# Reordering loads, transposes and casts in three blocks of a chunked-attention + squared-ReLU FFN kernel

## The chip, the cores and the metric

The kernel runs on one core of one Trainium2 chip. The metric is the device time of one execution in microseconds (us); lower is better. PE is the matmul engine (TensorE), DVE is VectorE, ACT is ScalarE, POOL is GpSimd, and SP is the engine whose queue issues nearly all DMAs here.

## The reference

The inputs are `q`, `k`, `v` of shape (8, 8, 576, 64) = (batch B, heads H, tokens S, head size D) and two weights, all float32. Attention is cut into chunks of 64 tokens that do not see each other; the result, 4608 tokens of 512 values, goes through a feed-forward layer with a squared ReLU.

```python
scores = scale * np.matmul(q_c, k_c.transpose(0, 1, 2, 4, 3))      # q_c, k_c, v_c: (B, H, 9, 64, D)
scores = scores - np.max(scores, axis=-1, keepdims=True)
attn = np.exp(scores)
attn = attn / (np.sum(attn, axis=-1, keepdims=True) + 1e-09)
out = np.matmul(attn, v_c)
x = out.transpose(0, 2, 1, 3).reshape(B * S, H * D)                # 4608 x 512
h = np.maximum(x @ w_in, 0.0)                                      # w_in 512 x 2048
return (h * h @ w_out)                                             # w_out 2048 x 512
```

## The kernel before

**Groups and blocks.** The 4608 tokens are cut into 18 groups of 256 tokens (four chunks), and the groups into 9 blocks of two: block j holds groups 2j and 2j+1. The FFN of block j is computed on PE while the attention of block j+1 (`nxt`) is fitted between its matmuls and the inputs of block j+2 (`far`) are loaded, cast and transposed. So block 3 holds groups 6 and 7, block 4 groups 8 and 9, block 5 groups 10 and 11.

**Steps of one group g.**
- Loads, all on SP's DMA queue: `qk_pieces` (L106, L120) gives one q load of 512 KB and two k loads of 256 KB (whole groups); `v_pieces` (L148, L152) gives two `ve_sb` loads of 128 KB (even heads) and two or three `vo_sb` loads of 64 or 128 KB (odd heads).
- `C` = `cast_q` (L334) and `cast_k` (L341): q and k to bf16, on POOL for g < 8, on ACT from there. `CQ` and `CK` are the two apart.
- `TD` = `transpose_qk_dma` (L352): one DMA transpose, also on SP's queue, gives `qkT`.
- `SC` = `scores` (L375 matmuls on PE, one exp on ACT, L386).
- `AV` = `values` (L403 matmuls on PE; reciprocal L410 and product L411 on DVE give `x`).
- `XT` = `transpose_x` gives `xT`, which the FFN reads: for g < 6 eight transposes on PE (L430) and one copy (L435); from g = 6 a DMA transpose on SP's queue (L424).

**The FFN of a block.** First comes x @ w_in (`ffn_in` or `ffn_in_unit`: matmuls L607 and, in blocks 2 to 8, the products of `unit`, L494), with the ReLU on ACT (L571, L598) and squares on DVE, POOL or ACT. Then `ffn_out` (L664): seven products into two PSUM banks, `n` and `m`, with copies of a bank to SBUF between them: n1 (L728), n2 (L737), and the output part (L771), all on ACT. The second product into `n` must wait until n1 is copied, the third until n2 is copied.

**The order** is written out by hand (`tc.manual_schedule()`): each engine and the queue run their instructions in the order in which the Python code emits them. A block is a list of *slots*; a slot is one `yield` of the FFN generators (four matmuls of 512 columns, or eight of 256). `plan` says which attention step is emitted after which slot; in each slot of `go_slots` one more load of the list `loads` is emitted, ahead of that slot's steps; loads that are left go out after the block's last slot. Block 1 has 46 slots (32 of `ffn_in`, 14 of `ffn_out`), blocks 2 to 8 have 33 (19 and 14). `late_by` is 3 in the blocks 2 to 8. In block j = 3 the casts of group 11 thus stand at the slots 21 and 22, and the steps SC of the next block's groups at slot 8; the SC of groups 10 and 11 stand at slot 4 of block 4. The stores of outputs of blocks 1 and later are put back (`late`) and issued on SP's queue (L715).

**The queue.** Every DMA adds to one of eight semaphores in turn, and each waits for the landing of the DMA eight places ahead of it, so at most eight are in flight.

Of the kernel before, what the change touches and what calls it, by code (L numbers as in the profile page):

```python
# [17 lines left out]
def kernel(  # L18
# [31 lines left out]
    def is_whole(g):  # L50
        return chunks[g][0][0] == chunks[g][3][0]
# [38 lines left out]
    def runs(g):  # L90

        for t in range(2):
            (b, s), (b1, s1) = chunks[g][2 * t:2 * t + 2]
            if b == b1:
                yield t, 0, 2 * CH, b, s
            else:
                yield t, 0, CH, b, s
                yield t, CH, CH, b1, s1

    def qk_pieces(g):  # L100
        q_sb = in_pool.tile([128, 2, H, D], FP32, name="q_sb")
        k_sb = in_pool.tile([128, 2, H, D], FP32, name="k_sb")
        qk[g] = (q_sb, k_sb)

        def pairs(dst, src, p, m, b, s):
            return lambda: nc.sync.dma_start(  # L106
                out=dst.rearrange("p t h d -> p (t h d)")[p:p + m // 2, :].rearrange(
                    "p (h e) -> p h e", h=H),
                in_=src[b, :, s:s + m, :].rearrange("h (s i) d -> s h (i d)", i=2))

        if is_whole(g):
            yield pairs(q_sb, q, 0, GT, *chunks[g][0])
        else:
            for c in range(4):
                yield pairs(q_sb, q, c * CH // 2, CH, *chunks[g][c])
        if g < FIRST_DMA_T:
            yield pairs(k_sb, k, 0, GT, *chunks[g][0])
            return
        for t, p, m, b, s in runs(g):
            yield lambda t=t, p=p, m=m, b=b, s=s: nc.sync.dma_start(  # L120
                out=k_sb[p:p + m, t, :, :],
                in_=k[b, :, s:s + m, :].rearrange("h s d -> s h d"))
# [23 lines left out]
    def v_pieces(g):  # L146
        for t, p, m, b, s in runs(g):
            yield lambda t=t, p=p, m=m, b=b, s=s: nc.sync.dma_start(  # L148
                out=v_even[g % NV][p:p + m, t, :, 0:D],
                in_=v[b, 0::2, s:s + m, :].rearrange("h s d -> s h d"))  # L150
        for n, p, m, b, s in odd_loads[g]:
            yield lambda n=n, p=p, m=m, b=b, s=s: nc.sync.dma_start(  # L152
                out=v_odd[n % NO][p:p + m, :, 0:D],
                in_=v[b, 1::2, s:s + m, :].rearrange("h s d -> s h d"))

    def go(pieces):
        for f in pieces:
            f()
# [278 lines left out]
    C, CQ, CK, TD = cast_qk, cast_q, cast_k, transpose_qk_dma  # L437
    SC, AV, XT = scores, values, transpose_x
# [183 lines left out]
    def sum_quarters(out, in0, in1, op=ALU.add, half=slice(None)):  # L622
        return lambda _: add(nc.vector, out[:, half], in0[:, half], in1[:, half], op)
# [182 lines left out]
    def pieces(grps):  # L806
        for g in grps:
            yield from qk_pieces(g)
        for g in grps:
            yield from v_pieces(g)  # L810
# [62 lines left out]
    for j, grps in enumerate(blocks):  # L873
        nxt = blocks[j + 1] if j + 1 < len(blocks) else []
        far = blocks[j + 2] if j + 2 < len(blocks) else []
        plan = {}

        def at(slot, f, g):
            plan.setdefault(slot, []).append((f, g))

        if j == 0:
            loads, go_slots = pieces(far), range(17)
            at(28, sum_quarters(b11_p_b21, b11, b21), None)
            for slot, f in ((24, TA), (27, SC), (29, AV), (31, XT)):
                at(slot, f, nxt[0])
            at(31, TQ, nxt[1])
            at(31, TK, nxt[1])
            at(31, sum_quarters(b11_m_b22, b11, b22, ALU.subtract), None)
            phases = [first_ffn_in, ffn_out_by_ft(0)]
        elif j == 1:  # L890
            loads, go_slots = itertools.chain(*map(qk_pieces, far)), range(26, 48)
            for slot, f in ((4, SC), (8, AV), (12, XT)):
                at(slot, f, grps[1])
            for i, g in enumerate(nxt):
                for slot, f in ((16 + 4 * i, C), (21 + 4 * i, TD), (36 + i, SC), (38 + 2 * i, AV),
                                (41 + 2 * i, XT)):
                    at(slot, f, g)
            for i, g in enumerate(far):
                at(36 + 4 * i, C, g)
                at(42 + 3 * i, TD, g)  # L900
            at(2, sum_quarters(b11_p_b12, b11, b12), None)
            at(12, sum_quarters(b12_p_b22, b12, b22), None)
            at(20, sum_quarters(b21_p_b22, b21, b22), None)
            phases = [ffn_in(1, [(0, 256, FT_ORDER), (256, 256, FT_ORDER)]), ffn_out(1)]
        else:
            loads, go_slots = pieces(far), range(32)
            slots = {SC: (4, 4), AV: (7, 11), XT: (10, 14), C: (18, 22), TD: (20, 24)}
            if j == 3:
                slots.update({SC: (8, 8), AV: (10, 14), XT: (13, 17)})
                go_slots = [*range(6), *range(13, 17), *range(20, 32)]  # L910
            if not is_whole(nxt[0] if nxt else 0):
                slots.update({SC: (6, 8), AV: (10, 14), XT: (12, 16)})
            if j == 2:
                loads = itertools.chain(*map(v_pieces, nxt), loads)
                slots = {SC: (8, 10), AV: (12, 15), XT: (15, 18), C: (20, 23), TD: (22, 25)}
                go_slots = [*range(16), *range(25, 36)]
            late_by = 0
            if j in UNITS:
                late_by = 3
            if j == 2:  # L920
                slots.update({AV: (12, 16), XT: (15, 19)})
                go_slots = [*range(16), *range(28, 39)]
            elif j in UNITS:
                go_slots = range(35)
                if far and is_whole(far[0]):
                    go_slots = [*range(6), *range(13, 17), *range(23, 35)]
                slots.update({SC: (4, 4), AV: (8, 13), XT: (12, 17)})
                if j == 3 or not is_whole(nxt[0] if nxt else 0):
                    slots.update({SC: (8, 8), AV: (11, 16), XT: (14, 19)})
            for f in (SC, AV, XT):  # L930
                for i, g in enumerate(nxt):
                    at(slots[f][i], f, g)
            if j > 2 and far and is_whole(far[0]):
                for slot, f, i in ((16, CQ, 0), (18, CK, 0), (18, TD, 0), (18, CQ, 1),
                                   (19, CK, 1), (19, TD, 1)):
                    at(slot + late_by, f, far[i])
            else:
                for f in (C, TD):
                    for i, g in enumerate(far):
                        at(slots[f][i] + late_by, f, g)  # L940
            phases = [ffn_in_unit(j) if j in UNITS else ffn_in(j, [(0, BT, FT_ORDER)]),
                      ffn_out(j)]
        slot = 0
        for phase in phases:
            for _ in phase:
                if slot in go_slots:
                    for f in loads:
                        f()
                        break
                for f, g in plan.get(slot, []):  # L950
                    f(g)
                while late and (slot >= LATE_STORES.get(j, 99) or (j, slot) == (2, 9)):
                    late.pop(0)()
                slot += 1
        assert all(x < slot for x in plan), (j, slot, sorted(plan))
        go(loads)
        while late and j > 1:
            late.pop(0)()
# [30 lines left out]
```

## Time and profile before

| | |
|---|---|
| time, median of 3 runs | 280.36 us (279.69 to 280.68) |
| the profiled execution | 282.07 us, span of its instructions 280.3 us |
| PE busy | 269.5 us (96%), 3047 matmuls |
| DVE, ACT, POOL busy | 205.2, 155.7, 95.4 us |
| DMA | 57.11 MB; SP's queue fills 84.8% of 16 DMA engines' span |
| granted PE clock | 0.993 on the mean |

The views name a group of instructions by line, engine, operation and tiles (out<-in), and say after `<-` what ended the idle time before it. `SPq` rows are the issuing of a DMA by SP's queue: their duration is the time to issue, and the landing comes later. The busy digits are tenths of a slice of 7 us.

### The profile page before, as it was taken

Reading aid. Unit: us, or ns where it says so; the run is one execution under the profiler, and the core shown is the slowest. Engines: PE = TensorE matmul, PEld = TensorE weight load, DVE = VectorE, ACT = ScalarE, POOL = GpSimd, SP = SyncE. Lnnn points to the kernel's source line nnn. Section 1 sums busy time; section 2 is a strip of 40 time slices with the busy share of each in tenths; the row PEclk is TensorE's granted clock in tenths of the full one; section 3 lists DMA queues with packets and bytes.
Section 4 is the critical chain, followed back from the end, with each engine's and each line's share of the span. In section 5 each row is a group of like instructions: output and inputs, shape, how many; then the busy total and the mean of one; then the engine's idle time right before and its main releaser. Section 6 shows DMA issues by size and latency. Waiting matters only on the chain.

```text
span 280.3 us, 7376 instructions
## 1 busy us (share of the span) xinstructions
PE 269.5 (96%) x3047; PEld 186.2 (66%) x3047; DVE 205.2 (73%) x313; ACT 155.7 (56%) x262; POOL 95.4 (34%) x110
## 2 busy tenths in 40 slices
PE   6987999999999999899999999999999999999995
PEld 4642445788785678457855785578558855885684
DVE  0542704899888798689868795979589949786794
ACT  1544713787426765579265927583779185507710
POOL 2036868351043810172017301720190019003403
PEclk9997999999999999999999999999999999999999
DMA  6999999989999879999999999897699992204004
GB/s 230 234 337 336 303 347 243 310 223 214 181 223 170 208 234 205 246 272 235 204 212 267 219 186 294 190 153 165 152 295 224 180 274 39 40 22 130 0 0 152
DMA packets 141313, 57.11 MB, mean 204 GB/s; under 512 B 110368, under 2 KB 135200, under 8 KB 141280
## 3 DMA queue, kind: packets, MB, share of 16 engines
q1 hardware_dynamic: 140544, 54.67, 84.8%
q0 software_dynamic: 592, 1.84, 1.7%
q8 instruction: 24, 0.39, 0.6%
q10 hardware_dynamic: 144, 0.13, 0.1%
q14 instruction: 9, 0.07, 0.1%
HBM read 36.70 MB, written 9.44 MB: 165 GB/s over the span
## 4 chain that ended last, share of the span: by engine, by line
PE 50%; DVE 0%; issue 0%
PE ps_ffn L664 24%; PE ps_ffn L607 19%; PE ps_ffn L494 6%; PE ps_att L403 1%; PE ps_att L375 1%; DVE o_sb L769 0%
## 5 line engine op out<-in xcount | busy, mean ns | idle before, releaser
L607 PE MATMUL ps_ffn<-xT,w_in_bf 128*128 128x512 bf16 (+1 forms) x528 | 112.7, 357 | 2.9 <-POOL w_in_bf L166 2.0
L620 POOL TENSOR_TENSOR gT<-rl 128x512 bf16<-128x512 f32 x40 | 45.5, 1152 | 121.5 <-ACT rl L571 118.3
L607 PEld LDWEIGHTS <-w_in_bf 128*128 128x128 bf16 x528 | 50.9, 99 | 40.8 <-POOL w_in_bf L166 2.5
L664 PEld LDWEIGHTS <-w_st 128*128 128x128 bf16 x640 | 62.2, 98 | 7.7 <-issue 0.4
L571 ACT ACTIVATE rl<-ps_ffn 128x512 f32<-128x512 f32 x84 | 50.0, 596 | 30.4 <-PE ps_ffn L607 30.2
L620 DVE TENSOR_TENSOR w_st<-gT 128x2048 bf16<-128x2048 bf16 x40 | 47.4, 1219 | 6.0 <-ACT gT L574 5.9
L664 PE MATMUL ps_ffn<-w_out_bf,w_st 128*128 128x256 bf16 x384 | 45.1, 273 | 0.0
L620 DVE TENSOR_TENSOR gT<-rl 128x512 bf16<-128x512 f32 x30 | 20.7, 691 | 21.1 <-ACT rl L571 20.7
L664 PE MATMUL ps_ffn<-w_sum,w_st 128*128 128x256 bf16 x256 | 29.6, 273 | 0.2 <-ACT n L737 0.2
L664 PEld LDWEIGHTS <-gT 128*128 128x128 bf16 x256 | 24.7, 98 | 5.0 <-ACT gT L574 0.5
L602 DVE TENSOR_TENSOR gT<-rl 128x256 bf16<-128x256 bf16 (+1 forms) x41 | 18.5, 491 | 10.2 <-ACT rl L598 9.8
L598 ACT ACTIVATE rl<-ps_ffn 128x256 bf16<-128x256 f32 (+1 forms) x48 | 20.3, 455 | 9.6 <-PE ps_ffn L607 8.9
L511 DVE SCALAR_TENSOR_TENSOR gT<-rl 128x512 bf16<-128x512 f32 x21 | 23.2, 1103 | 0.4
L411 DVE TENSOR_TENSOR x<-ps_att,rec 128x512 bf16<-128x512 f32 x32 | 22.1, 691 | 1.1
L771 ACT COPY o_sb<-ps_ffn 128x512 f32<-128x512 f32 x7 | 4.1, 585 | 30.4 <-PE ps_ffn L664 30.4
L386 ACT ACTIVATE e<-ps_att 128x1024 bf16<-128x1024 f32 x16 | 15.8, 1023 | 5.4 <-PE ps_att L375 5.4
L494 PEld LDWEIGHTS <-w_dif 128*128 128x128 bf16 x140 | 13.1, 98 | 7.5
L664 PE MATMUL ps_ffn<-w_out_bf,gT 128*128 128x256 bf16 x128 | 15.6, 273 | 0.0
L664 PE MATMUL ps_ffn<-w_sum,gT 128*128 128x256 bf16 x128 | 15.3, 273 | 0.0
L166 POOL CAST w_in_bf<-w_st 128x1024 bf16<-128x1024 f32 (+1 forms) x9 | 8.7, 969 | 19.0 <-DMA w_st<-in_moe_w_in_dram 19.0
L620 DVE TENSOR_TENSOR w_st<-xT 128x1024 bf16<-128x1024 bf16 (+1 forms) x21 | 12.5, 652 | 2.8 <-DMA xT<-x 2.0
L781 PE MATMUL ps_ffn<-w_out_bf,gT 128*128 128x512 bf16 x64 | 14.5, 380 | 0.0
(82 smaller groups left out, 294.2 us busy)
## 6 DMA issues: line engine op xcount, KB each, us to landing
q_sb<-in_q_dram SPq DMA_DIRECT2D x16, 512.0 KB, 6.4
k_sb<-in_k_dram SPq DMA_DIRECT2D x24, 256.0 KB, 6.0
out_dram<-o_sb SPq DMA_DIRECT2D x12, 512.0 KB, 4.3
w_st<-in_moe_w_in_dram SPq DMA_DIRECT2D x8, 512.0 KB, 8.6
w_st<-in_moe_w_out_dram SPq DMA_DIRECT2D x8, 512.0 KB, 6.0
ve_sb<-in_v_dram SPq DMA_DIRECT2D x28, 128.0 KB, 3.2
vo_sb<-in_v_dram SPq DMA_DIRECT2D x21, 128.0 KB, 3.1
k_sb<-in_k_dram SPq DMA_DIRECT2D x4, 512.0 KB, 6.8
```

Of the source, the lines that this page charges most:

```text
L166: nc.gpsimd.tensor_copy(out=w_in_bf[:, :, i * 256 + c:i * 256 + c + n], in_=st[:, :, c:c + n])
L386: nc.scalar.activation(out=e_out, in_=s_in, func=AF.Exp, scale=scale)
L411: nc.vector.tensor_tensor(out=x[:, t].rearrange("p h a d -> p a h d"), in0=o[:, :, :, 0:D], in1=rec.to_broadcast([128, 2, n_hp, D]), op=AL ...
L494: nc.tensor.matmul(out=out[:, 256 * f:256 * f + 256], lhsT=a[:, d, 128 * f:128 * f + 128], rhs=b[:, :, d, :], start=(first and f == 0 and ...
L511: later.append(lambda: nc.vector.scalar_tensor_tensor(out=place_of(i, jj), in0=both(x), scalar=0.0, in1=both(x), op0=ALU.max, op1=ALU.mult))
L571: nc.scalar.activation(out=rl, in_=h, func=AF.Relu)
L598: nc.scalar.activation(out=rl[:, 0:n], in_=h[:, 0:n], func=AF.Relu)
L602: nc.vector.tensor_tensor(out=gT[:, ft, c:c + n], in0=rl[:, 0:n], in1=rl[:, 0:n], op=ALU.mult)
L607: nc.tensor.matmul(out=h[:, 0:n], lhsT=w_in_bf[:, dt, ft * 128:(ft + 1) * 128], rhs=xT[:, c // 128:(c + n) // 128, dt, :], start=(dt == 0) ...
L620: engine.tensor_tensor(out=out, in0=in0, in1=in1, op=op)
L664: nc.tensor.matmul(out=outs[t], lhsT=a[:, i, t * 128:(t + 1) * 128], rhs=b[:, i, :], start=(first and i == 0 and (last or t == 0)), stop=( ...
L781: nc.tensor.matmul(out=o_ps[tt], lhsT=gT[:, ft, tt * 128:(tt + 1) * 128], rhs=w_out_bf[:, ft, :], start=(ft == 0), stop=(ft == n_ft - 1))
```

## The change

Three places of the main loop, where the slots are given out.

- In block 0, the loads are q,k of groups 4 and 5 and V of group 4 alone; V of group 5 (four loads) goes to the head of block 1's list, which starts at slot 26. As the DMA transposes of groups 4 and 5 stand at the slots 21 and 25 of block 1, these now come before V of group 5 on SP's queue. In block 1 the transposes of x of group 3 on PE move from slot 12 to slot 13.
- In block 2, the queue's slots are 0 to 11, 20 to 22, and 28 on, in place of 0 to 15 and 28 on. On SP's queue the q and k loads of group 9 (and one V load of group 8) thus move from ahead of the two DMA transposes of x of groups 6 and 7 (slots 15 and 19) to behind them.
- In block 3, the casts of group 11 and its DMA transpose move from the slots 21 and 22 to 25 and 26. On ACT the two casts come behind the copy n2 (L737), which they stood ahead of. On SP's queue the transpose of group 11 comes behind four V loads (one of group 10, three of group 11) that it stood ahead of.

```diff
         if j == 0:
-            loads, go_slots = pieces(far), range(17)
+            loads = itertools.chain(*map(qk_pieces, far), v_pieces(far[0]))
+            go_slots = range(17)
...
         elif j == 1:
-            loads, go_slots = itertools.chain(*map(qk_pieces, far)), range(26, 48)
-            for slot, f in ((4, SC), (8, AV), (12, XT)):
+            loads = itertools.chain(v_pieces(nxt[1]), *map(qk_pieces, far))
+            go_slots = range(26, 48)
+            for slot, f in ((4, SC), (8, AV), (13, XT)):
                 at(slot, f, grps[1])
...
             if j == 2:
                 slots.update({AV: (12, 16), XT: (15, 19)})
-                go_slots = [*range(16), *range(28, 39)]
+                go_slots = [*range(12), *range(20, 23), *range(28, 39)]
...
             if j > 2 and far and is_whole(far[0]):
-                for slot, f, i in ((16, CQ, 0), (18, CK, 0), (18, TD, 0), (18, CQ, 1),
-                                   (19, CK, 1), (19, TD, 1)):
+                q1, k1 = (22, 23) if j == 3 else (18, 19)
+                for slot, f, i in ((16, CQ, 0), (18, CK, 0), (18, TD, 0), (q1, CQ, 1),
+                                   (k1, CK, 1), (k1, TD, 1)):
                     at(slot + late_by, f, far[i])
```

## The prediction

> **What bounds the kernel now.** The page comes first.
>
> ```profile
> PE 269.5 (96%) x3047; PEld 186.2 (66%) x3047; DVE 205.2 (73%) x313; ACT 155.7 (56%) x262; POOL 95.4 (34%) x110
> ...
> PE   6987999999999999899999999999999999999995
> ...
> DMA  6999999989999879999999999897699992204004
> ```
>
> PE is the bound: after the start it is nearly always busy. But the DMA row is as full as PE's until about 230 us, so transfers are a second conveyor that runs neck and neck with PE. Next, who PE itself waited for.
>
> ```profile
> PE ps_ffn L607 <- DMA xT<-x: 0.9, 1, 0.9
> ...
> PE ps_att L375 <- DMA qkT<-qkb: 0.5, 1, 0.5
> PE ps_att L430 <- DVE x L411: 0.4, 1, 0.4
> ...
> PE ps_ffn L664 <- ACT n L737: 0.2, 1, 0.2
> ```
>
> Apart from waits in the first 30 us this is all: four waits, each near one of the edits. Their places are in PE's timeline.
>
> ```profile
> 59.90 0.40 PE L430 MATMUL ps_att<-ident,x 128*128 128x128 bf16 x4 [0.38 <-DVE x L411]
> ...
> 71.92 1.04 PE L664 MATMUL ps_ffn<-w_out_bf,w_st 128*128 128x256 bf16 x8
> 72.96 0.45 PE L375 MATMUL ps_att<-qkT 64*64 64x64 bf16 x32
> 73.34 1.05 PE L664 MATMUL ps_ffn<-w_out_bf,w_st 128*128 128x256 bf16 x8
> 74.89 0.45 PE L375 MATMUL ps_att<-qkT 64*64 64x64 bf16 x32 [0.51 <-DMA qkT<-qkb]
> ```
> ```profile
> 106.79 3.66 PE L664 MATMUL ps_ffn<-w_sum,w_st 128*128 128x256 bf16 x32
> 110.29 1.91 PE L664 MATMUL ps_ffn<-w_out_bf,w_st 128*128 128x256 bf16 x16
> 113.10 2.76 PE L607 MATMUL ps_ffn<-xT,w_in_bf 128*128 128x512 bf16 x12 [0.90 <-DMA xT<-x]
> ...
> 131.96 3.66 PE L664 MATMUL ps_ffn<-w_out_bf,w_st 128*128 128x256 bf16 x32
> 135.87 3.65 PE L664 MATMUL ps_ffn<-w_sum,w_st 128*128 128x256 bf16 x32 [0.25 <-ACT n L737]
> ```
>
> The idle figures count from a matmul's modelled end, which overlaps the next start when nothing waits, so they are too small. I count by starts: 32 matmuls from 106.79 to 110.29 are 0.109 each. The fifth view is the queue, just where the third edit puts four V loads ahead of a transpose.
>
> ```profile
> 135.55 1.26 SPq L424 DMA_TRANSPOSE xT<-x  x1
> 136.91 4.60 SPq L352 DMA_TRANSPOSE qkT<-qkb  x2
> 141.56 0.57 SPq L152 DMA_DIRECT2D vo_sb<-in_v_dram  x1
> 142.19 1.05 SPq L148 DMA_DIRECT2D ve_sb<-in_v_dram  x2
> 143.28 1.18 SPq L152 DMA_DIRECT2D vo_sb<-in_v_dram  x2
> ```
>
> The queue issues without a pause. The second L352 row is group 11: its 2.37 us of issuing start at 139.14 and it lands 4.5 us on, at 143.6. Its reader, the second half of the 64 L375 matmuls that start at 145.09, starts at 145.42. So it is 1.8 us early.
>
> **The change part by part.**
>
> *Transposes of x of group 3, one slot later: 0.0.* The second four wait for x (DVE L411, 59.15 + 0.69 = 59.84). One slot is 4 matmuls, 0.44, so most of the 0.38 goes. But they still cannot start before 59.9, and the ACT copy behind them (60.33, 1.01 long) still ends at 61.3 to 61.4. The first matmul that reads it comes 12 matmuls after 60.13 now, at 61.44, just in time; then only 8 stand between, PE is there at 61.0, and it waits 0.4 for the same copy. The stall changes place. Bounds: gain 0.4 (nothing waits on the copy) to loss 0.1 (one relu, 0.37, now stands ahead of the copy).
>
> *V of group 5 behind the transposes of groups 4 and 5: gain 0.8.* The four loads took the queue from 64.52 to 66.95, 2.4 us; the transposes go earlier by that, except that the second needs the cast of k (POOL, 64.19 + 1.10 = 65.29), which still permits 3 us. It landed 6.1 after 68.78, at 74.85, and 2.4 less is 72.4. PE would be at the second scores at 73.34 + 8 x 0.109 = 74.22 and was there at 74.89: 0.67. The first scores add 0.16 (71.92 + 0.87 = 72.80 against 72.96). V of group 5 lands some 5 us later, at about 74; its reader (AV, 78.6) has 4 us to spare. Bounds: 0.5 (the idle alone) to 0.8.
>
> *x of groups 6 and 7 ahead of q,k of group 9: gain 1.05.* The two transposes started at 106.7 behind 7.3 us of issuing (q 99.31 to the V load's end 106.59). Their x was there at 97.8 and 101.4 (DVE). They now land by about 107, and block 3 need not wait: 110.29 + 16 x 0.109 = 112.04 against the row at 113.10. In return k of group 9 lands two transposes later. The two landed 0.84 apart (106.70 + 5.5 and 108.37 + 4.7), so they take some 1.8 of conveyor time: the last k load lands at about 111.2, not at 109.4 (104.04 + 5.4), and its cast on ACT (1.04) ends at 112.3, behind which L771 and block 3's first relus stand. They are due at 112.2 or later, so some 0.1 to 1 us of delay on ACT, covered by the four PSUM banks. The transpose of group 9 follows the cast and lands at 117 to 118; its reader is at 120.03, 1.9 earlier by the gains, so the cover is thin (0 to 0.5 us lost, and then the gain is smaller). One store (landing 1.25 apart from the load ahead of it) also passes a V load of group 8, which then lands at about 120.8 for a reader at 122.2 that comes 1.85 earlier: up to 0.5. Bounds: 0 to 1.05.
>
> *n2 ahead of the casts of group 11: gain 0.4.* L737 stood behind the last cast (134.28 + 1.05) and PE behind L737: 131.96 + 32 x 0.109 = 135.46 against 135.87. The casts come 0.6 later at most, and the transpose behind them is later still, so they hide.
>
> Together PE would reach block 4's scores 0.8 + 1.05 + 0.4 = 2.25 us earlier, at 142.84 and 143.17.
>
> *The transpose of group 11 behind four V loads: this sets the end.* The four issues run from 141.51 to 143.78 without a gap: 2.27 us. So the transpose starts at 141.4 and lands at 143.6 + 2.27 = 145.9. PE now wants it at 143.17: it waits 2.7 us. Against before (145.42) that is 0.45 us later. The earlier gains do not enter this figure at all: PE waits for the queue, and whatever it won is waited away. From there PE's order is as it was and later blocks have no DMA wait in the trace of before, so nothing gives the loss back.
>
> Two terms move the landing. First, a 16 KB packet of the instruction queue (24 of them, "q8 instruction") holds up one of the 16 DMA engines. One falls in the V loads here (the second L148 landed after 4.1 us, the one ahead of it after 2.9: +1.2). With PE some 2 us ahead it comes at about 142.4, into the flight of the transpose instead. At 71 us it cost more: the first transpose landed 6.0 after its start, against 4.5 and 4.9 here, and the DMA moved 75 and 77 GB/s in the two us from 71 to 73, against 274 at 69. Bounds 0 to 1.6; I take 0.9. Second, the conveyor itself can be earlier or later than in this trace: earlier because the 71 us hold-up hits V loads rather than a transpose that blocks the queue (up to 1), later because the cast of group 9 holds its transpose (up to 0.6). I take 0.4 earlier. Sum: 0.45 + 0.9 - 0.4 = +0.95 us.
>
> [...]
>
> The profiled execution took 282.07 (span 280.3 and 1.8 around it), 0.6% above the median of 280.36. I add the sum to the median: 281.3. An execution without the profiler may have less DMA delay, and then less of each stall, wins and loss alike; this goes into the chances.
>
> **The rivals.**
>
> *Faster: the transpose lands in time (0.15).* If the queue is over 1.3 us ahead of before when it gets to the transpose (issue before about 140.1), the landing is before 144.6 and over 0.84 us of the 2.25 stays; with 2.7 ahead all of it does, 278.1. For it: the freed time at 66.95 to 73.07. Against it: no row of the queue from 121 to 141 shows a pause that a shift could fill.
>
> *No change (part of 0.33).* The DMA waits at 74 and 113 are largely the profiler's; then only the 0.4 of n2 is to be had and the transpose is late by little: -0.4 to +0.5, 280.0 to 280.9.
>
> *Much slower (part of 0.52).* The 16 KB packet costs its full 1.6 and the conveyor is 0.3 to 0.6 late, since the cast of group 9 holds the queue: 0.45 + 1.6 + 0.45 = +2.5, 282.9.
>
> *The first edit does not do what it says:* the stall at 59.9 only moves to 61. This is in the forecast at nothing; if I am wrong it gives 0.4 before the bottleneck, which then swallows it.
>
> **How the numbers follow.** A measurement of this kernel can tell about 0.3%, 0.84 us, from no change. My forecast, the late transpose with a sum of +0.3 to +1.9, has 0.60, of which 0.40 lies above 0.84; much slower 0.12; no change 0.13; faster 0.15. So slower 0.40 + 0.12 = 0.52, same 0.20 + 0.13 = 0.33, faster 0.15. The predicted time is 281.3. The range runs from 279.1 (into the faster case, most of which, about 0.12, stays out) to 282.7 (0.06 above).
>
> **What would show it.** Right: PE's list has lost the waits for xT and for L737, and has one new long wait, L375 <- DMA qkT, of 2 to 4 us four slots into block 4, with the second transpose of the pair behind four V rows; the wait at 59.9 is replaced by one at L607 for the copy L435. The step on the queue is wrong if that wait is under 1.5 us; the step on group 9 is wrong if PE waits over 0.5 us at block 3's scores or ACT's L771 starts more than 1 us after its product. The whole is wrong if the transpose of group 11 lands before PE is there: then the time is under 279.

## The result, and the profile after

| | before | after |
|---|---|---|
| time, median | 280.4 us (279.69 to 280.68, 4 runs) | 283.6 us (282.62 to 284.29, 4 runs) |
| the profiled execution | 282.07 us, span 280.3 | 283.28 us, span 281.5 |
| PE busy | 269.5 us | 268.5 us |

The ratio is 1.0115 (95% interval 1.0078 to 1.0152): 3.2 us slower, where 0.95 was forecast and the range ended at 2.3 above before. The direction held, the size did not. (Ratios here and below leave disturbed executions out, so they can differ from a ratio of medians or means: most in e5 below, where 2 of 12 are left out and the means of all give 0.9976.)

First, PE's list of waits in the changed kernel: line waited at, who was waited for, total us, times, longest.

```profile
PE ps_att L375 <- DMA qkT<-qkb: 2.9, 1, 2.9
...
PE ps_att L403 <- DMA vo_sb<-in_v_dram: 0.5, 1, 0.5
...
PE ps_ffn L607 <- DMA xT<-x: 0.3, 1, 0.3
...
PE ps_ffn L607 <- ACT xT L435: 0.2, 1, 0.2
```

All four waits of before are gone (L607 for x of groups 6 and 7, L375 at 74 us, L430, L664 for n2). In their place stand the forecast wait for the transpose of group 11, the stall for the copy L435 that took the place of L430's, and two that the sum had at nothing: V of group 8 (`vo_sb`), which was only in the bounds of a step, and x of group 9. PE's timeline around the long wait:

```profile
141.53 0.45 PE L375 MATMUL ps_att<-qkT 64*64 64x64 bf16 x32
144.88 0.44 PE L375 MATMUL ps_att<-qkT 64*64 64x64 bf16 x32 [2.90 <-DMA qkT<-qkb]
145.25 0.95 PE L494 MATMUL ps_ffn<-w_st,w_in_bf 128*128 128x256 bf16 x4
145.99 1.91 PE L607 MATMUL ps_ffn<-xT,w_in_bf 128*128 128x512 bf16 x4
```

The last two rows are the surprise: four matmuls of L607 take 1.91 us here, and 1.03 in a slot at full clock. The windows of the same stretch (interval, its length, busy share of each engine with its count, then PE's granted clock, DMA share and GB/s) say why:

```profile
143.00:144.00 1.00, 0.00 (x0) 0.00 (x0) 0.00 (x0) 0.15 (x1) 0.00 (x0) 1.00 1.10 250
...
145.00:146.00 1.00, 1.00 (x37) 0.76 (x34) 0.00 (x0) 0.61 (x1) 0.00 (x0) 0.69 1.05 404
146.00:147.00 1.00, 1.00 (x4) 0.45 (x3) 0.69 (x1) 0.41 (x1) 0.00 (x0) 0.50 1.07 332
147.00:148.00 1.00, 1.00 (x5) 0.39 (x4) 0.00 (x0) 0.06 (x1) 0.00 (x0) 0.50 0.82 187
148.00:149.00 1.00, 1.00 (x6) 0.62 (x5) 0.43 (x1) 0.69 (x2) 0.00 (x0) 0.60 1.08 323
```

Just after the wait PE is granted half its clock for about 3.4 us, in which it does 1.7 us less of work. The profile of before had the same event in another place: a wait of 2.0 us for `w_in_bf` at 21 us, and then a clock of 0.50 from 24 to 27 us. Most executions do not have such a start: of before's 145 timed runs beside the experiments, 26 have a mean clock of 0.994 or less. The sum was made against it.

The queue, as predicted, has the second L352 row behind four V rows (L152, two L148, L152):

```profile
134.49 1.99 SPq L352 DMA_TRANSPOSE qkT<-qkb  x1
136.53 0.57 SPq L152 DMA_DIRECT2D vo_sb<-in_v_dram  x1
137.15 1.07 SPq L148 DMA_DIRECT2D ve_sb<-in_v_dram  x2
138.27 0.51 SPq L152 DMA_DIRECT2D vo_sb<-in_v_dram  x1
138.87 2.44 SPq L352 DMA_TRANSPOSE qkT<-qkb  x1
```

It lands 5.96 us after its start, at 144.83. The DMA view of the window from 141 to 144 us (40 slices of 0.075 us) shows where the flight went: from the tenth GB/s figure on, the engines move 0 to 14 GB/s for 19 slices, 1.4 us, and one instruction packet of 16 KB (queue q8) is in the window, from 141.3 to 142.3 us.

```profile
DMA  9999999999000000010000000010699999999999
GB/s 259 225 253 461 239 270 266 276 256 3 0 0 0 0 0 0 3 10 7 7 10 10 7 10 10 7 14 7 137 287 283 297 294 283 290 294 287 294 287 290
...
q8 instruction: 1, 0.02, 2.1%
```

### The profile page after: what moved, and what is told of

Its sections match the earlier page's. It is cut to its first block, busy times and chain, and to the rows that moved or that the text cites. A ratio compares the mean times of both kernels' runs of the same rounds, so it can differ in the third digit from the quotient of the medians.

```text
span 281.5 us, 7374 instructions
## 1 busy us (share of the span) xinstructions
PE 268.5 (95%) x3044; PEld 185.5 (66%) x3047; DVE 204.6 (73%) x313; ACT 155.9 (55%) x262; POOL 95.9 (34%) x110
## 4 chain that ended last, share of the span: by engine, by line
PE 69%; DMA 16%; SPq 7%; DVE 4%; ACT 1%; POOL 1%; issue 1%
PE ps_ffn L664 30%; PE ps_ffn L607 28%; PE ps_ffn L494 8%; DMA w_st<-in_moe_w_in_dram 5%; DMA qkT<-qkb 4%; SPq L237 3%; DMA k_sb<-in_k_dram 2%; DMA w_st<-in_moe_w_out_dram 2%; PE ps_att L403 2%; SPq L152 2%; DMA xT<-x 2%; DMA vo_sb<-in_v_dram 1%; DVE w_st L620 1%; PE ps_att L375 1%; DVE x L411 1%
## 5 line engine op out<-in xcount | busy, mean ns | idle before, releaser
L607 PE MATMUL ps_ffn<-xT,w_in_bf 128*128 128x512 bf16 (+1 forms) x528 | 112.4, 356 | 1.2 <-POOL w_in_bf L166 0.5
L607 PEld LDWEIGHTS <-w_in_bf 128*128 128x128 bf16 x528 | 50.6, 98 | 39.0 <-POOL w_in_bf L166 2.1
L664 PEld LDWEIGHTS <-w_st 128*128 128x128 bf16 x640 | 62.2, 98 | 7.3
L664 PE MATMUL ps_ffn<-w_out_bf,w_st 128*128 128x256 bf16 x384 | 45.1, 273 | 0.0
L664 PE MATMUL ps_ffn<-w_sum,w_st 128*128 128x256 bf16 x256 | 29.6, 273 | 0.0
L664 PEld LDWEIGHTS <-gT 128*128 128x128 bf16 x256 | 24.7, 98 | 5.0 <-ACT gT L574 0.5
L664 PE MATMUL ps_ffn<-w_out_bf,gT 128*128 128x256 bf16 x128 | 15.6, 273 | 0.0
L664 PE MATMUL ps_ffn<-w_sum,gT 128*128 128x256 bf16 x128 | 15.3, 273 | 0.0
```

Of the source, the lines that this page charges most:

```text
L607: nc.tensor.matmul(out=h[:, 0:n], lhsT=w_in_bf[:, dt, ft * 128:(ft + 1) * 128], rhs=xT[:, c // 128:(c + n) // 128, dt, :], start=(dt == 0) ...
L664: nc.tensor.matmul(out=outs[t], lhsT=a[:, i, t * 128:(t + 1) * 128], rhs=b[:, i, :], start=(first and i == 0 and (last or t == 0)), stop=( ...
```

## The experiments

Theory A: the four V loads ahead of the transpose of group 11 are the loss. Rivals: B, the loss is in the first two edits (V of group 8, x of group 9); C, it is the clock behind the wait. Every kernel below except b2 was run twelve times (e4 six times), side by side with the kernel before, and every ratio is to that.

### The change taken apart: e1, e2, e5, e6, e15, e16

**e1**, the change without its third edit:

```diff
-                q1, k1 = (22, 23) if j == 3 else (18, 19)
...
+                for slot, f, i in ((16, CQ, 0), (18, CK, 0), (18, TD, 0), (18, CQ, 1),
+                                   (19, CK, 1), (19, TD, 1)):
```

> The changed kernel with the third edit taken back (casts and transpose of group 11 at their old places), the first two kept. Theory A (the transpose of group 11 behind four V loads makes the loss): the wait of 2.9 us in block 4 is gone, the 0.4 us for the copy n2 comes back, the gains of the first two edits stay (0.5 to 1.9 us): 278.5 to 279.9, and no half clock around 146 us. Theory B (the first two edits hold the queue up: late V of group 8, late xT of group 9): the time stays above 281, with waits of 0.5 us and more at L403 and at block 4's first L607.

Measured: 1.0041 (1.0011 to 1.0070). Most of the loss is gone with the third edit, but the gain that two edits should have left is not there: they lose 0.4%, and the median of 280.97 lies in neither theory's range. PE's largest wait after the start is now this one:

```profile
PE ps_ffn L664 <- ACT n L737: 1.7, 1, 1.7
```

**e2**, before with the third edit alone.

> The kernel before with the third edit alone. Theory A: the transpose of group 11 starts 2.3 us later and lands 2.2 to 3.7 us later, so PE waits 0.8 to 2.3 us at the second scores of block 4; with 0.4 won at n2: 280.8 to 282.5, and up to 1.7 more in an execution where the wait brings a window of half clock. Theory B: within 0.3% of before, since PE has 1.8 us to spare there and 0.4 more is won: 279.9 to 280.5.

Measured: 1.0105 (1.0074 to 1.0137), nearly the whole 1.0115. With the V loads ahead, PE waits for the transpose whatever the first two edits did. Theory A holds for the loss of the change. Rival B is not nothing: the first two edits lose 0.41% when they stand alone (e1), but 0.41 and 1.05 do not add up to the 1.15 of the change, so most of that loss does not show when PE has to wait for the transpose anyway.

**e5**, before with the first edit alone, and **e6**, with the second alone (the `go_slots` of block 2).

> Before plus the first edit alone: V of group 5 behind the transposes of groups 4 and 5, transposes of x of group 3 one slot later. Forecast of the prediction: the wait for qkT at 74 us is gone, gain 0.5 to 0.8 us, ratio 0.997 to 0.998. Rival (PE cannot keep a lead, because the casts of group 11 and the copy n2 behind them wait for the queue, which is not earlier): 0 to -0.2 us, ratio 0.999 to 1.000, with the wait at L737 longer by what was gained. Rival (V of group 5 behind the transposes puts the queue's later work off): slower by 0.2 to 0.4 %.

> Before plus the second edit alone: q and k of group 9 and one V load of group 8 behind the transposes of x of groups 6 and 7. Forecast of the prediction: the wait for xT at 113 us is gone, gain 1.05 us, ratio 0.996. Rival (the step on group 9 is wrong: the transpose of group 9 is held on the queue until its k is cast, and V of group 8 and the loads of groups 10 and 11 stand behind it): the xT wait is replaced by L403 <- DMA vo_sb of 0.7 to 2.5 us near 119 us or by L664 <- ACT n L737 of 1 to 2 us near 132 us, and the time is 0 to 1.5 us above before, ratio 1.000 to 1.005.

Measured: e5 0.9953 (0.9924 to 0.9981), e6 1.0023 (0.9988 to 1.0058). The first edit gains, as forecast or more (e10 below, which contains it, has 0.9957). The second does not: e6 cannot be told from nothing, but with the first edit it loses (e1, 1.0041, against e5: the intervals do not meet). In the waits of e6 the one for `xT` is gone, and two have come that together are larger:

```profile
PE ps_ffn L664 <- ACT n L737: 1.2, 1, 1.2
...
PE ps_att L403 <- DMA vo_sb<-in_v_dram: 0.8, 1, 0.8
```

**e15** and **e16**, the two halves of the first edit: V of group 5 alone, and the transposes of x alone (`(12, XT)` against `(13, XT)`).

> Of the first edit only V of group 5 behind the transposes of groups 4 and 5; the transposes of x of group 3 stay at slot 12. By the sum of the prediction it has the whole gain of the first edit, 0.5 to 0.8 us: ratio 0.997 to 0.998, or 0.9953 as the first edit whole. If the gain was that of the transposes of x, it is 0.999 to 1.001.

> Of the first edit only the transposes of x of group 3 one slot later. By the sum 0.0: the stall of 0.4 us for x (DVE L411) becomes one for the copy (ACT L435), ratio 0.999 to 1.001, and the waits L430 <- DVE x and L607 <- ACT xT together stay at 0.4 to 0.6 us. If it has a part of the first edit's gain, the ratio is 0.997 to 0.998 and the two waits are 0.2 us or less together.

Measured: e15 0.9988 (0.9959 to 1.0018), e16 1.0011 (0.9982 to 1.0040). Neither can be told from nothing, nor e15 from the 0.9953 of the whole edit. In e16 the stall went from L430 to L607 behind L435 (0.2 us), as forecast. What share each has of the first edit's gain stays open.

### How many loads the transpose can bear: e3, e7, e11, e13

**e3**, the change with the V loads of block 3 held until the transpose of group 11 has been issued:

```diff
                     go_slots = [*range(6), *range(13, 17), *range(23, 35)]
+                    if j == 3:
+                        go_slots = [*range(6), *range(13, 17), *range(27, 35)]
```

> The changed kernel, casts of group 11 behind n2 as in the change, but the four V loads (and the fifth) wait until the transpose of group 11 is on the queue. Theory A: all three gains and no wait: 278.1 to 279.5, 0 to 0.4 below the kernel without the third edit. Theory B: above 281.

Measured: 1.0044 (1.0013 to 1.0074), the same as e1: with the V loads behind it, the rest of the third edit costs nothing. The wait for the transpose is gone, and the largest is V of group 8:

```profile
PE ps_att L403 <- DMA vo_sb<-in_v_dram: 2.5, 1, 2.5
```

**e7**, before with the casts behind n2 and the same V loads held.

> Before plus only the good half of the third edit: the casts of group 11 and their transpose behind the copy n2, but the four V loads held back until the transpose has been issued. If the V loads ahead of the transpose are the whole cost of the third edit, nothing of its 1.05 % is left, and the 0.4 us forecast for n2 shows: ratio 0.998 to 0.999 (0.3 to 0.6 us faster), no wait L375 <- DMA qkT over 0.7 us between 140 and 148 us. If the later casts themselves are the cost, the ratio is 1.005 or more and that wait is 1.5 us or more. If V of group 10 becomes late by being held (readers at block 4's values, some 4 us behind the scores), a wait L403 <- DMA vo_sb or ve_sb of 0.5 us or more appears near 150 us.

Measured: 1.0000 (0.9970 to 1.0031). So the V loads are all of the third edit's cost, and the copy n2 ahead of the casts gains nothing that shows. e7 and e2 differ in the V loads alone, which makes them the pair to read the lateness from. The queue and PE in e7:

```profile
135.08 4.54 SPq L352 DMA_TRANSPOSE qkT<-qkb  x2
139.68 0.57 SPq L152 DMA_DIRECT2D vo_sb<-in_v_dram  x1
```
```profile
142.14 0.71 PE L375 MATMUL ps_att<-qkT 64*64 64x64 bf16 x64
```

and in e2:

```profile
139.63 2.03 SPq L352 DMA_TRANSPOSE qkT<-qkb  x1
```
```profile
145.34 0.45 PE L375 MATMUL ps_att<-qkT 64*64 64x64 bf16 x32 [2.45 <-DMA qkT<-qkb]
```

In e7 the second transpose is issued at 137.12 and lands at 141.64, 0.8 us before the second half of PE's 64 matmuls (142.41). In e2 it is issued at 139.63 and lands at 145.29: 2.51 us later at the queue, and 1.14 more in flight.

**e11** and **e13**, before with the casts and the transpose two and three slots later, which puts two and three V loads ahead of it in place of four:

```diff
-                for slot, f, i in ((16, CQ, 0), (18, CK, 0), (18, TD, 0), (18, CQ, 1),
-                                   (19, CK, 1), (19, TD, 1)):
+                q1, k1 = (20, 21) if j == 3 else (18, 19)
+                for slot, f, i in ((16, CQ, 0), (18, CK, 0), (18, TD, 0), (q1, CQ, 1),
+                                   (k1, CK, 1), (k1, TD, 1)):
```

(e13 has `(21, 22)`.)

> Before, with the casts and the transpose of group 11 two slots later, so that two of the four V loads are ahead of the transpose and not four (the casts are still ahead of n2). Each load takes the queue some 0.57 us, so the transpose should land 1.1 to 1.3 us later than without any, at 142.7 to 143.0 by the spans of the other runs, and PE is there at 142.4 to 142.7: a wait of 0 to 0.6 us, no stage at half clock behind it, ratio 1.000 to 1.003. If the cost of the third edit goes with the number of loads and has no threshold, it is half of 1.05 %: 1.005.

> Before, with the casts and transpose of group 11 three slots later: three of the four V loads ahead of the transpose, and only the last cast behind n2. Two loads gave 0.9998 with the landing at 141.99 and PE there at 142.5 to 142.7, four gave 1.0105 with the landing at 145.29. At 0.57 us of issuing for a load plus up to 1.1 us of longer flight, the landing should be 142.6 to 144.2 and the wait 0 to 1.5 us: ratio 1.000 to 1.005. If the fourth load is what makes the step (a wait of over 2 us, and the half clock behind it), three cost at most 0.3 %; if the price is in proportion to the loads, 0.8 %.

Measured: e11 0.9998 (0.9967 to 1.0029), e13 1.0068 (1.0033 to 1.0103).

| V loads ahead | kernel | issued | landed | flight | PE waits | ratio |
|---|---|---|---|---|---|---|
| 0 | e7 | 137.12 | 141.64 | 4.5 | 0 | 1.0000 |
| 2 | e11 | 137.75 | 141.99 | 4.2 | 0 | 0.9998 |
| 3 | e13 | 138.80 | 144.84 | 6.0 | 2.2 | 1.0068 |
| 4 | e2 | 139.63 | 145.29 | 5.7 | 2.5 | 1.0105 |

The price sets in between two loads and three: two hide under the slack, and the third makes the flight longer by 1.8 us as well as the issue later by 1.05. (Between three loads and four the intervals overlap, so whether it is flat or rises from there is not shown.) In e13, as in the changed kernel, the DMA all but stops for about a microsecond ahead of the landing (5 to 10 GB/s from 143.25 to 144.25 us), with a 16 KB instruction packet at 142.55. In e7 a shorter stop lies at 138.75 to 139.5, in the flight of both transposes; the instruction packet just ahead of it is one of 8 KB, of another queue (q14, at 138.31). The window is 136 to 146 us, in slices of 0.25:

```profile
GB/s 260 216 243 197 264 292 286 288 275 258 201 24 7 23 252 230 290 293 287 292 198 163 209 205 265 136 217 215 236 260 102 34 16 122 182 422 392 385 410 410
...
q14 instruction: 1, 0.01, 0.2%
```

e7's transpose of group 11 flew 4.5 us through that stop, and the 16 KB packet came at 142.12, after its landing. In e11 that packet came at 141.47, only 0.5 us ahead of the landing, and there is no stop between 136 and 146 us. The traces of all 19 profiles together carry this further. Of the 264 q and k transposes whose landing is known, the 82 with no instruction packet in flight took 3.7 to 4.6 us (median 4.0), the 38 with an 8 KB packet alone 4.3 to 5.1 (4.8), and the 144 with a 16 KB packet 3.7 to 6.8 (5.5). By these traces the third load pushes the transpose into a packet that it escapes behind two. That the packet itself causes the stop is argued from this, since no run took it away.

### The clock: e4 and e12

**e4**, the change with PE kept busy ahead of the late scores:

```diff
+        if g == 11:
+            keep_busy(24, ps)
```

> The changed kernel with 24 extra matmuls on the identity (2.6 us) written to the PSUM bank of group 11's scores ahead of them, so PE works instead of waiting. Theory C (part of the loss is the half clock after the wait, 3.41 us at 0.5 in the trace of the changed kernel, 1.7 us): no half-clock window near 146 us in any execution and a time 0.8 to 1.7 us below the changed kernel, about 282. Theory A alone: the same time as the changed kernel (283.6, within 0.4), as PE still cannot start the scores before the transpose lands. If the extra matmuls outlast the wait: up to 0.6 us slower.

Measured: 1.0102 (1.0055 to 1.0149), no better than the change. It does not decide, since in its profile another wait appeared, 1.6 us for V of group 8 (with no slow stage behind it there), and the mean clock of its six runs, 0.9935, is no higher than that of e2. **e12** repeats it on e2, whose blocks 1 and 2 are those of before.

> Before plus the third edit, with 24 extra matmuls (2.6 us) of no use on PE between the scores of group 10 and those of group 11, where PE had waited 2.5 us. The transpose is as late as with the third edit alone, PE starts the scores of group 11 at the same time, but is not idle. If a stage at half clock behind the wait is part of the 1.05 %, the mean granted clock rises from 0.994 to 0.998 and the ratio falls to 1.004 to 1.007. If the wait alone is the cost, the ratio stays 1.009 to 1.012. Where the transpose is less late than 2.6 us the filler itself costs up to 2.6.

Measured: 1.0083 (1.0054 to 1.0112), 0.2% under e2, but the intervals overlap, and it lies between the two ranges expected. The mean granted clock of each execution is sharper: a stage of 3.4 us at half clock makes it 0.994.

| kernel | mean clock over its runs | runs at 0.994 or less |
|---|---|---|
| before (beside e1 to e4) | 0.9984 | 5 of 29 |
| before (beside e12 and e13) | 0.9988 | 4 of 29 |
| before (beside e11) | 0.9977 | 10 of 35 |
| e2, third edit alone | 0.9940 | 9 of 12 |
| e13, three loads ahead | 0.9945 | 9 of 12 |
| e12, e2 with the wait filled | 0.9971 | 4 of 12 |
| e11, two loads ahead | 0.9980 | 3 of 12 |

So with the wait the slow stage is there in most executions, not in all (e2's own profile has it nowhere: 1.00 throughout after its 2.45 us), and it does not need that wait: in the profiles of e6, e10, e11 and e14 (mean clocks 0.992, 0.992, 0.994 and 0.988) a stage lies at 11 to 19 us. Worked out from the means, (0.9984 - 0.9940) x 280 = 1.2 us of e2's loss is clock at most. The times say less than that. In e2 the three runs at 0.998 or more took 281.7 us on the mean, 2.1 above before's 24 such runs (279.6), and the six at 0.994 took 283.6; but in e13 the two means are 281.4 and 281.7, and the changed kernel's one run at full clock, 284.29 us, is the slowest of its four. So Theory C alone is not it: e2 without a slow stage is still some 2 us behind. How much of the rest is the clock, between nothing and 1.2 us, is not shown.

### The second edit: e8, e9, e10, e14, and before once more

**Before, profiled again**, to see whether the waits that the gains were read from are always there.

> The kernel before, unchanged, profiled a second time, because its first profile had lost 3 us in the first 27 us (a wait of 2.0 us for w_in_bf and 3.4 us at half clock behind it) that the kernels profiled since did not lose. If the gains forecast for the first two edits are real, the waits L375 <- DMA qkT (0.5) and L607 <- DMA xT (0.9 idle, 1.05 by starts) are here again or larger, since PE is up to 3 us earlier and the queue is not. If they were accidents of that one execution, they are gone. The rival that PE's lead is simply waited away elsewhere asks for a longer wait at L737 or L375 between 130 and 145 us here.

Measured: this execution lost time at the start too (mean clock 0.988, waits of 1.9 us for q and 1.7 for `w_in_bf`), so it does not answer for a clean start. But the waits for `qkT` at 74 us and for `xT` at 113 us are not in its list. In the kernels that share blocks 1 and 2 with before, the wait for `xT` runs from 1.1 (e2) over 0.5 (e7) and 0.4 (e13) to none over 0.2 (e11): it is no fixed 1.05.

**e8**, the first two edits with V of group 8 earlier on the queue:

```diff
-                go_slots = [*range(12), *range(20, 23), *range(28, 39)]
+                go_slots = [*range(12), *range(20, 39)]
```

> The first two edits without the third, with the five V loads of group 8 issued ahead of the wait for the cast of group 9 (three of them ahead of the transpose of group 8, two between the two transposes). If the second edit costs because V of group 8 was left behind the held transpose of group 9 and a store, the wait L403 <- DMA vo_sb near 119 us cannot come back, and the time falls from the 1.0041 of the first two edits toward the 0.9953 of the first alone: 0.995 to 0.999. If the cost is elsewhere (the casts of group 11, which wait for the queue whatever is done before, so that PE's lead is waited away at L664 <- ACT n L737), the wait at L737 of 1.5 to 2 us stays and the ratio with it, 1.002 to 1.005. The forecast of the prediction for the two edits together, 1.85 us, would be 0.993.

Measured: 0.9973 (0.9946 to 0.9999), where e1 had 1.0041. V of group 8 was the second edit's cost. But there is no gain over the first edit alone: the next reader waits for the transpose of group 9, which now stands behind V:

```profile
118.67 0.45 PE L375 MATMUL ps_att<-qkT 64*64 64x64 bf16 x32 [1.25 <-DMA qkT<-qkb]
```

**e9**, all three edits with both repairs (those of e3 and e8).

> All three edits with both suspected costs taken out: V of group 8 ahead of the held transpose of group 9, and the four V loads of block 3 behind the transpose of group 11. If these two are the whole loss of 1.15 %, the gains that the prediction gave to the edits are left, 1 to 2.25 us: ratio 0.992 to 0.997, no wait of PE for a DMA over 0.7 us after 60 us. If edits two and three gain nothing even so, it stands with the first edit alone, 0.995 to 0.997. If the transposes or V of groups 8 to 10 become the next to be late, a wait L375 or L403 <- DMA of over 1 us shows and the ratio is 1.000 or more.

Measured: 0.9981 (0.9951 to 1.0010), with the same wait of 1.3 us. The two repairs take away the whole 1.15% of loss, and nothing of the forecast gain of 2.25 us is left above what the first edit gives.

**e10**, the first edit and e7.

> The first edit (0.9953 alone) and the casts of group 11 behind n2 with the V loads held (1.0000 alone). If the copy n2 behind the casts is what waits away a lead of PE (L664 <- ACT n L737, 0.84 us by starts with the first edit alone), this gains another 0.4 to 0.8 us: ratio 0.992 to 0.995. If the late casts make the transpose of group 11 the next to be late, L375 <- DMA qkT of 0.5 us or more shows near 143 us and the ratio is 0.995 to 0.998.

Measured: 0.9957 (0.9924 to 0.9989). It is faster than before by some 0.4%, like e5, and so the n2 half again adds nothing that shows. e5 and e10 are the versions that beat both kernels most clearly; e8's interval ends at 0.9999.

**e14**, e10 with one transpose of x ahead of the k loads of group 9, and V of group 8 no later than before:

```diff
-                go_slots = [*range(16), *range(28, 39)]
+                go_slots = [*range(13), 16, 17, 20, 21, *range(28, 39)]
```

> The first edit with n2 and the transpose of group 11 ahead of V (0.9957), and of the second edit only this much: the first transpose of x ahead of the two k loads of group 9, the second behind them, and V of group 8 not later than before. If the second edit fails only because V of group 8 and the transpose of group 9 become late, the wait for xT near 111 us (1.1 to 1.4) shrinks to 0.5 or less and nothing takes its place: 0.992 to 0.995. If the conveyor of the queue decides and every wait taken away comes back at the next reader, it stays at 0.995 to 0.997 with a new wait L375 <- DMA qkT or L403 <- DMA vo_sb of 1 us between 115 and 125 us.

Measured: 0.9982 (0.9951 to 1.0012). Its waits:

```profile
PE ps_att L375 <- DMA qkT<-qkb: 0.8, 1, 0.8
PE ps_ffn L607 <- DMA xT<-x: 0.7, 1, 0.7
```

The wait for x, 1.1 in e10, shrank by less than half, and e14 is no better than e10. In this stretch the queue decides, as far as these orders show it: each that served one reader earlier served another later.

## Why the prediction was right and wrong, step by step

**Transposes of x of group 3: 0.0. Right.** The stall is at L607 behind the copy L435 now, and e16 cannot be told from before.

**V of group 5: 0.8 gained. Right in sign, its size open.** Both waits for `qkT` near 74 us are gone (PE has no idle between 69 and 76 us), and the first edit gave 0.47% (0.2 to 0.8%), 1.3 us. But the wait that the 0.8 was read from is no fixed one, since b2, e11 and e13, which have before's order here, do not list it; and this part alone (e15) cannot be told from nothing.

**x of groups 6 and 7: 1.05 gained. Wrong, and in sign where the first edit is in (e1 against e5).** The wait for `xT` at 113 us did go. But the step gave the price of V of group 8 as "up to 0.5", by the store alone. It had missed that both `ve_sb` loads of group 8 moved one place back: the first from ahead of the transposes of x to behind the transpose of group 8, and with that the second from there to behind the transpose of group 9, which is held for its cast. Before, the queue ran thus:

```profile
112.90 0.58 SPq L148 DMA_DIRECT2D ve_sb<-in_v_dram  x1
113.59 1.97 SPq L352 DMA_TRANSPOSE qkT<-qkb  x1
115.61 1.82 SPq L152 DMA_DIRECT2D vo_sb<-in_v_dram  x3
117.53 0.46 SPq L715 DMA_DIRECT2D out_dram<-o_sb  x1
```

The queue of the changed kernel shows both, the pause between the first two rows and the V and store rows behind it:

```profile
109.19 0.58 SPq L148 DMA_DIRECT2D ve_sb<-in_v_dram  x1
110.50 1.59 SPq L352 DMA_TRANSPOSE qkT<-qkb  x1
112.13 0.58 SPq L148 DMA_DIRECT2D ve_sb<-in_v_dram  x1
112.76 1.26 SPq L152 DMA_DIRECT2D vo_sb<-in_v_dram  x2
114.12 0.45 SPq L715 DMA_DIRECT2D out_dram<-o_sb  x1
114.66 0.42 SPq L152 DMA_DIRECT2D vo_sb<-in_v_dram  x1
```

The last V load of group 8 lands at 119.70 in e6 against 117.01 in e5: 2.7 us later, not 1.25. PE waits 0.5 to 2.5 us for it in the profiles of the change, e3, e4 and e6, though not in that of e1. And where V is mended, the gain is still not there (e8, e9).

**n2 ahead of the casts: 0.4 gained. Not confirmed.** The wait at L737 is gone in the changed kernel, but e7 is at 1.0000, and e10 is no faster than e5.

**The transpose of group 11: net 0.45 + 0.9 - 0.4 later. The right mechanism, mis-sized: the step that failed.** The wait forecast, 2.7 us (3.2 with the two terms of the landing), is 2.90 in the profile, and the remark that PE's earlier gains would be waited away held: the change is as slow as e2, which has none of them. The net failed. The sum set a lead of 2.25 us against that wait, which left 0.45, and the runs show no such lead: the first two edits alone are 0.41%, 1.1 us, slower (e1) where 1.85 us were to be won, and n2 alone won nothing that shows (e7). The same seen from the queue, by e2 against e7:
- The shift of the landing was put at 2.27 + 0.9 - 0.4 = 2.77. It is 2.51 + 1.14 = 3.65: nothing of the 0.4 came, and the flight was longer than the 0.9. The packet term behind the 0.9 was right in kind: the 16 KB packet did come into the flight (in the changed kernel from 141.3 to 142.3 us, in a flight from 138.87 to 144.83). The profile of before has 24 such packets with 0.6% of the 16 engines' span, which makes 1.1 us of one engine for each.
- The slack was read as 1.8 us from one execution. It is 0.8 in e7, where PE does not wait for n2, 1.6 to 1.9 in e1, e5 and e6, and 3.2 in before's second profile. What before has in a common execution stays open.
- The clock behind the wait, up to 1.2 us on the mean, was not in the sum, although the profile of before showed the very event, at 24 to 27 us behind a wait of 2.0 us.

The wait is then 3.65 less a slack of 0.8 to 1.9, so 1.8 to 2.9 us, and up to 1.2 of clock comes on top. Measured for the third edit were 1.05%, 2.1 to 3.8 us by its interval, where the three terms of the sum had 0.95. How much of the difference is slack and how much is clock stays open.

The stages at half clock lasted 3.4 us and came behind waits of 2.0 (before), 2.2 (e13), 2.5 (e3) and 2.9 us (the change), so in a sum for this kernel a wait of 2 us must be counted as one that may cost 1.7 more (an estimate: half of the 3.4).

**The base.** The sum was made against one execution that had lost 3 us in its first 27 us. Later profiles without that loss have PE at block 4's scores at 142.1 to 142.5 us (e2, e7, e11), not at 145.09. The waits of 0.25 to 1.05 us read from it were taken as if every execution had them.

## What to carry to other kernels

Where one queue is nearly as full as the bound engine (here 84.8% of the DMA engines' span against PE's 96%), a wait that is taken away by reordering the queue can be paid at the next reader, as in e6, e8, e9 and e14; list, for every transfer that is passed, its reader and slack, the one or two small loads included. A transfer moved behind others cost nothing while the slack lasted (two loads ahead, 0.9998), and beyond it the wait (2.2 us in e13, 2.5 in e2, 2.9 in the change) and, in two of these three profiles (e13 and the change), a stage of 3.4 us at half clock. Take the slack from two or three profiles, and look at the first stage of each to see whether the execution was a clean one.

## What the runs showed of the hardware

Half clock came behind waits of PE of 2.0 (before), 2.2 (e13), 2.5 (e3) and 2.9 us (the change), and lasted 3.4 us each time; behind 2.45 us (e2) and behind 1.6 to 1.8 us (e1, e4, and e13 at 21 us) it did not come. In before's second profile (mean clock 0.988) a stage of 6.8 us began inside a wait of 1.7.

In the changed kernel the DMA all but stopped (0 to 14 GB/s) for 1.4 us ahead of the late transpose's landing, with a single instruction packet of 16 KB in the window. The flight of a q and k transpose goes with such packets, over 264 flights in the 19 profiles: median 4.0 us with none in flight, 4.8 with one of 8 KB, 5.5 with one of 16 KB.
